# Pooled attention and rational MoE on one core: a planner with other costs and a table of due times, one-row scalars, a second home for q, 128-row last key chunk

## The chip, the cores and the metric

The kernel runs on one core of one Trainium2 chip. The metric is device time in microseconds of one execution. Engines: TensorE (PE in the profile; its weight loads are PEld), VectorE (DVE), ScalarE (ACT), GpSimd (POOL) and SyncE (SP), which here only issues DMAs.

## What is computed

```python
# q, k, v: 8 batches x 8 heads x 576 x 64, fp32
k_p = k.reshape(B, H, 72, 8, D).mean(axis=3)         # keys and values pooled by 8
v_p = v.reshape(B, H, 72, 8, D).mean(axis=3)
scores = scale * np.matmul(q, k_p.transpose(0, 1, 3, 2))
attn = np.exp(scores - np.max(scores, axis=-1, keepdims=True))
attn = attn / (np.sum(attn, axis=-1, keepdims=True) + 1e-09)
x = np.matmul(attn, v_p)                              # as 4608 tokens x 512
h = x @ w_in                                          # 512 x 2048
P = a[0] + a[1] * h + a[2] * h2 + a[3] * h3           # h2 = h*h, h3 = h2*h
Q = 1.0 + np.abs(b[0]) * np.abs(h) + np.abs(b[1]) * h2
out = (P / (Q + 1e-6)) @ w_out                        # 2048 x 512
```

## The kernel before

The 4608 tokens are 18 blocks of 256, each of two tiles of 128 tokens. The 2048 hidden columns are 8 units of 256. For a block, attention makes x in two parts (a rounded one and the remainder, since the fp32r matmul keeps fewer bits); for a block and a unit, mm1 makes h in the PSUM tile ph (24 matmuls of 128x256), rational makes gh and gl from it on ScalarE, VectorE and GpSimd, and mm2 adds them into two PSUM tiles po (12 matmuls of 128x512). Weights (win, wout) are loaded once as raw words (rwin, rwout), split into two parts on chip and kept.

In the names of the profile: st_k, st_v, and for the first two batches early, hold raw k and v; ks the pooled keys; pk (four chunks) and pl (the fifth, of 64 rows) are their transposes in PSUM, kpT the copy in SBUF. The pooled values are vm (main) and vr (the remainder of 16 rows a head), for the first two batches by matmuls with the identity, pvs and pvr. For a tile, pq is the transpose of q and qT its copy; ps the scores, mx and sm the row maximum and the sum, e the exponentials; pm and pr are transposes of e, am (hi and lo) their copies; pv the value products, x their copy. Blocks 0 to 3 transpose on TensorE; later ones on VectorE and by DMA.

The code does not issue instructions as it runs. `Plan.add` (line 125) records each with an engine, a cost in us and what it depends on. `solve` (line 166) is a list scheduler: each engine in turn takes the operation that can start first by the recorded costs and, among those within `LOOK`, the one with the least due time. Due times come from a pace of units (`due`, line 889) less a slack along the dependences. `shift` (line 158) moves the due times of some 3% of the first 1850 operations by random amounts, for each of twelve seeds. `issue` (line 252) then writes the instructions engine by engine in that order. Wherever by the plan TensorE has a gap, it fills it with matmuls of no use (line 276): into the bank idle up to a marked place, and after it, of zeros, into an open po bank. The chip keeps each engine's order and waits on semaphores, whatever the plan's times were.

Of the scalars, a and b are loaded to 128 partitions with a broadcast (line 435), and GpSimd and ScalarE make the factors abn from them (lines 437 to 440). qT has one buffer (line 634). pl is made of 64 rows (lines 511 to 514). The scores of a tile are two operations, one for each half of the heads (line 657); a tile that spans two batches (4 of the 36) has twice the matmuls, each 64 tokens wide.

## Time and profile before

| | us |
|---|---|
| median of 3 runs | 944.13 (943.72 to 944.32) |
| span of the profiled execution | 943.9 |
| TensorE busy in it | 932.3 (99%) |
| VectorE, ScalarE, GpSimd busy | 786.0, 693.7, 528.0 |

The profiled execution's own time beyond its span is not recorded; its span is 0.2 us under the median. Busy time of TensorE holds the fillers, and its matmuls are pipelined: a row's mean duration is longer than the distance of two starts.

### The profile page before, as it was taken

Reading aid. Unit: us, or ns where it says so; the run is one execution under the profiler, and the core shown is the slowest. Engines: PE = TensorE matmul, PEld = TensorE weight load, DVE = VectorE, ACT = ScalarE, POOL = GpSimd, SP = SyncE. Lnnn points to the kernel's source line nnn. Section 1 sums busy time; section 2 is a strip of 40 time slices with the busy share of each in tenths; the row PEclk is TensorE's granted clock in tenths of the full one; section 3 lists DMA queues with packets and bytes.
Section 4 is the critical chain, followed back from the end, with each engine's and each line's share of the span. In section 5 each row is a group of like instructions: output and inputs, shape, how many; then the busy total and the mean of one; then the engine's idle time right before and its main releaser. Section 6 shows DMA issues by size and latency. Waiting matters only on the chain.

```text
span 943.9 us, 17079 instructions
## 1 busy us (share of the span) xinstructions
PE 932.3 (99%) x6152; PEld 845.0 (90%) x6152; DVE 786.0 (83%) x1336; ACT 693.7 (73%) x1124; POOL 528.0 (56%) x463
## 2 busy tenths in 40 slices
PE   8899999999999999999999999999999999999998
PEld 8888998989988899998999899998999899999996
DVE  7799988788989888887887997888898987887664
ACT  4788889868675877686776777676868595868674
POOL 4776866866446544445634574447545663544443
PEclk9999999999999999999999999999999999999999
DMA  9994201254235322122603160316222421202000
GB/s 275 313 390 160 45 29 46 67 127 87 49 81 105 86 34 47 29 56 53 138 5 75 51 140 8 54 37 139 47 36 50 97 50 28 51 1 57 1 23 23
DMA packets 185365, 75.33 MB, mean 80 GB/s; under 512 B 162624, under 2 KB 162624, under 8 KB 185280
## 3 DMA queue, kind: packets, MB, share of 16 engines
q1 hardware_dynamic: 185280, 74.23, 31.2%
q8 instruction: 49, 0.80, 0.4%
q14 instruction: 36, 0.29, 0.1%
HBM read 50.60 MB, written 12.58 MB: 67 GB/s over the span
## 4 chain that ended last, share of the span: by engine, by line
PE 87%; DMA 3%; SPq 3%; DVE 3%; POOL 1%; ACT 1%; issue 1%; POOLq 0%; ACTq 0%
PE ph L284 39%; PE po L284 39%; PE pv L284 4%; PE ps L284 4%; SPq L284 3%; DMA q<-in_q_dram 1%; DMA early<-in_v_dram 1%; DVE sm L284 1%; DMA st_v<-in_v_dram 1%; DVE t L284 1%; POOL w L284 0%; PE pvs L284 0%; ACT rp L284 0%; PE pq L284 0%; DVE mx L284 0%
## 5 line engine op out<-in xcount | busy, mean ns | idle before, releaser
L284 PEld LDWEIGHTS ph<-x,win 128*128 128x128 f32 x3264 | 472.7, 188 | 55.5 <-ACT w L284 0.8
L284 PE MATMUL ph<-x,win 128*128 128x256 f32 x3264 | 495.7, 282 | 1.4 <-DVE x L284 0.5
L284 PE MATMUL po<-wout,gh 128*128 128x512 f32 x1152 | 353.1, 397 | 0.1
L284 POOL TENSOR_TENSOR w<-w,r 128x512 f32<-128x512 f32 (+1 forms) x145 | 191.1, 1318 | 230.3 <-ACT r L284 228.1
L284 POOL TENSOR_TENSOR gl<-t,gh 128x512 fp32r<-128x512 f32 (+1 forms) x145 | 193.3, 1333 | 93.1 <-ACT gh L284 91.9
L284 PEld LDWEIGHTS po<-wout,gh 128*128 128x128 f32 x1152 | 185.7, 189 | 12.5 <-POOL wout L284 0.8
L284 PE MATMUL po<-wout,gl 128*128 128x512 f32 x576 | 181.8, 396 | 0.3 <-POOL gl L284 0.3
L284 ACT ACTIVATE rp<-w,cbias 128x512 f32<-128x512 f32 (+1 forms) x145 | 99.6, 687 | 59.8 <-POOL w L284 56.6
L284 DVE SCALAR_TENSOR_TENSOR t<-t,abn,rp 128x512 f32<-128x512 f32 (+1 forms) x145 | 107.3, 740 | 38.4 <-ACT rp L284 35.3
L284 DVE TENSOR_TENSOR t<-t,ph 128x512 f32<-128x512 f32 (+1 forms) x145 | 97.8, 675 | 48.7 <-ACT t L284 46.7
L284 ACT ACTIVATE r<-w,abn 128x512 f32<-128x512 f32 (+1 forms) x145 | 117.9, 813 | 20.8 <-POOL gl L284 11.4
L284 ACT ACTIVATE t<-ph,abn 128x512 f32<-128x512 f32 (+1 forms) x145 | 111.0, 767 | 26.3 <-PE ph L284 23.0
L284 ACT ACTIVATE w<-ph 128x512 f32<-128x512 f32 (+1 forms) x145 | 85.7, 591 | 40.8 <-PE ph L284 34.4
L284 DVE SCALAR_TENSOR_TENSOR t<-t,abn,ph 128x512 f32<-128x512 f32 (+1 forms) x145 | 107.0, 738 | 5.2 <-ACT w L284 1.3
L284 ACT CAST gh<-t 128x512 fp32r<-128x512 f32 (+1 forms) x145 | 88.3, 609 | 20.5 <-DVE t L284 16.9
L284 DVE SCALAR_TENSOR_TENSOR t<-rp,t 128x512 f32<-128x512 f32 (+1 forms) x145 | 99.4, 685 | 4.1
L284 DVE SCALAR_TENSOR_TENSOR rp<-w,rp 128x512 f32<-128x512 f32 (+1 forms) x145 | 99.0, 683 | 0.2
L284 PEld LDWEIGHTS po<-wout,gl 128*128 128x128 f32 x576 | 93.0, 189 | 6.4 <-POOL gl L284 0.5
L284 ACT ACTIVATE rp<-rp 128x512 f32<-128x512 f32 (+1 forms) x145 | 84.1, 580 | 3.6 <-DVE t L284 0.5
L284 POOL TENSOR_TENSOR e<-e,sm 128x576 f32<-128x576 f32 x36 | 41.8, 1175 | 51.2 <-DVE sm L284 38.7
L284 POOL TENSOR_TENSOR st_v<-st_v 128x512 f32<-128x512 f32 (+1 forms) x36 | 36.3, 1015 | 17.4 <-DMA st_v<-in_v_dram 10.7
L284 PE MATMUL ps<-kpT,qT 128*128 128x144 f32 (+1 forms) x320 | 45.6, 292 | 0.4 <-DVE kpT L284 0.2
(101 smaller groups left out, 855.9 us busy)
## 6 DMA issues: line engine op xcount, KB each, us to landing
am<-e SPq DMA_DIRECT2D x224, 48.0 KB, 2.1
out_dram<-ob SPq DMA_DIRECT2D x17, 512.0 KB, 3.1
rwin<-in_moe_w_in_dram SPq DMA_DIRECT2D x8, 1024.0 KB, 11.1
rwout<-in_moe_w_out_dram SPq DMA_DIRECT2D x8, 1024.0 KB, 14.1
st_k<-in_k_dram SPq DMA_DIRECT2D x12, 512.0 KB, 4.8
st_v<-in_v_dram SPq DMA_DIRECT2D x12, 512.0 KB, 4.2
q<-in_q_dram SPq DMA_DIRECT2D x144, 32.0 KB, 2.0
st_v<-in_v_dram SPq DMA_DIRECT2D x48, 64.0 KB, 2.2
```

What stands on the lines that cost most here:

```text
L284: getattr(engines[op.eng], name)(*map(value, args), **{k: value(v) for k, v in kw.items()})
```

## The change

The planner's costs are set anew: a lower fixed cost for VectorE and ScalarE (0.16 and 0.17 to 0.068 and 0.06), GpSimd 0.14 and 2.15 ns an element instead of 0.45 and 1.72, TensorE's costs by the operation; a result is ready `TAIL` after its operation's end and `HOP` later on another engine; loads move at 410 instead of 390 GB/s. `shift` uses a table, `LATER`, of due times by the operation's number, and `HOLD` gives seven operations an earliest start in the plan; both replace the random seeds. The attention of blocks 1 to 3 gets a due time 8 or 10 us earlier. a and b are loaded as one row each; a matmul with a row of ones, ab, spreads them over 128 partitions. The second tile's qT of blocks 0 and 1 lies in a part of early. The lower 64 rows of the last key chunk's ks are set to zero and all 128 rows are transposed. A two-batch tile's scores are one operation.

```diff
 class Plan:
-    LAT = 0.07
-    BEGIN = {"sp": 0.8, "pe": 1.7, "pool": 1.3, "dve": 1.5, "act": 1.5}
+    TAIL = {"sp": 0.0, "pe": 0.16, "pool": 0.06, "dve": 0.09, "act": 0.1}
+    HOP = {"sp": 0.035, "pe": 0.035, "pool": 0.08, "dve": 0.035, "act": 0.035}
+    BEGIN = {"sp": 0.8, "pe": 2.1, "pool": 1.3, "dve": 1.5, "act": 1.5}
-    MOVED, SHARE, REACH = 1850, 0.03, 4.0
-    SHIFTS = (600170, 650652, 293686, 721265, 222299, 972752, 932340, 238443, 467684, 409349, 642869, 707107)
+    RATE = 410e3
+    LATER = {
+        40: -21840.4, 45: -7931.8, 50: -6005.5, 61: -3867.9, 77: -7203.6, 85: -2.3, 99: -5839.5,
...
+    HOLD = {
+        80: 10.7, 85: 12.91, 94: 18.34, 135: 28.4, 183: 31.95, 216: 29.1, 458: 52.15,
+    }
     def shift(self):
+        for n, us in self.LATER.items():
+            self.ops[n].due += us
     def solve(self):
+            op.ready = max(op.ready, self.HOLD.get(op.seq, 0.0))
...
-                op.end = bus + 2.2
+                op.done = bus + 2.2
...
+                if u.eng != op.eng:
+                    u.ready = max(u.ready, op.done + u.lead + self.HOP[u.eng])
+                elif op.eng == "pe":
+                    u.ready = max(u.ready, op.end + u.lead)
+                else:
+                    u.ready = max(u.ready, op.done + u.lead + 0.03)
...
-    dve = Engine(plan, "dve", 0.16, 1.04)
-    act = Engine(plan, "act", 0.17, 0.85)
-    gp = Engine(plan, "pool", 0.45, 1.72)
+    dve = Engine(plan, "dve", 0.068, 1.04)
+    act = Engine(plan, "act", 0.06, 0.85)
+    gp = Engine(plan, "pool", 0.14, 2.15)
...
     def scalars():
-        dma(2, ab[:, 0:4], a.partition_broadcast(P))
-        dma(1, ab[:, 4:6], b.partition_broadcast(P))
+        small("memset", line, 1.0)
         for i in range(4):
-            small("tensor_scalar", out=abn[:, i:i + 1], in0=ab[:, i:i + 1],
-                                scalar1=-WS ** -i, scalar2=None, op0=ALU.mult)
-        act(6).activation(abn[:, 4:6], ab[:, 4:6], AF.Abs)
+            small("memset", scale[:, i:i + 1], -WS ** -i)
+        dma(0.02, ab[:, 0:4], a.unsqueeze(0))
+        dma(0.02, ab[:, 4:6], b.unsqueeze(0))
+        every = bank("ab", [P, 6])
+        pe(220, [mm(every, line, ab, True, True)])
+        dve(4).tensor_tensor(out=abn[:, 0:4], in0=every[:, 0:4], in1=scale[:, 0:4], op=ALU.mult)
+        act(6).activation(abn[:, 4:6], every[:, 4:6], AF.Abs)
...
-            ks = new("work1", "ks", [P, 2, 2, D], F32, f"ks{n}_{c0}")[:np, 0:nc_]
+            every = new("work1", "ks", [P, 2, 2, D], F32, f"ks{n}_{c0}")
+            ks = every[:np, 0:nc_]
+            if np < P:
+                gp(2 * D).memset(every[np:, 0:nc_], 0.0)
...
-                ("transpose", (pk[:, (c0 + c) * P:(c0 + c + 1) * P] if c0 < 4 else pl[:, 0:np],
-                               ks[:, c].rearrange("p a d -> p (a d)"), ident[:np, :np]), {})
+                ("transpose", (pk[:, (c0 + c) * P:(c0 + c + 1) * P] if c0 < 4 else pl,
+                               every[:, c].rearrange("p a d -> p (a d)"), ident), {})
...
-        qT = new("work1", "qT", [P, NJ * P], F32, f"qT{t}").rearrange("p (j t) -> p j t", j=NJ)
+        qT = (early(t // 2, 1)[:, RW:2 * RW] if t in (1, 3) else
+              new("work1", "qT", [P, NJ * P], F32, f"qT{t}")).rearrange("p (j t) -> p j t", j=NJ)
...
+        scores = [bank(f"ps{t}_{c}", [P, 4, SP]) for c in range(2)]
+        calls = [mm(scores[c][r0:r1, 2 * jj:2 * jj + 2, :], qT[:, 2 * c + jj, r0:r1],
+                    kpT[n % 2][:, 2 * c + jj, :], True, True)
+                 for c in range(2) for jj in range(2) for r0, r1, n in sg]
+        for part in [calls] if len(sg) > 1 else [calls[:2], calls[2:]]:
+            pe(1350 if len(sg) > 1 else 244 * 2, part, claims=(e, mx, sm))
...
+            plan.now = due(at) - (0 if again else {1: 8, 2: 10, 3: 10}.get(i, 0.0))
             xs[i, again] = reload(i, kept.pop(i)) if again else attend(i)
```

TensorE in the head, before: from the last scores of tile 1 to the first value products (pvs, pvr: pooled values of the first batch; idle x22: fillers).

```order
L284 MATMUL ps_0_258<-kpT_99,qT_243 128x144 x2
L284 MATMUL pvs_263<-early_2_116,identr 128x256 x8
L284 MATMUL pvr_289<-early_1_103,fourfold 128x128 x8
L284 MATMUL pm_308<-identr,e_240 128x128 x4
L284 MATMUL pm_316<-identr,e_240 128x128 x4
L276 MATMUL idle<-identr 128x256 x2
L284 MATMUL pr_331<-identr,e_240 128x128 x2
L276 MATMUL idle<-identr 128x256 x2
L284 MATMUL pr_344<-identr,e_240 128x128 x2
L276 MATMUL idle<-identr 128x256 x22
L284 MATMUL idle<-identr 128x128
L284 MATMUL pq_390<-identr,q_256 128x128 x4
```

The same place after.

```order
L307 MATMUL ps_0_249<-kpT_99,early_1_110 128x144 x2
L307 MATMUL pvs_258<-early_2_120,identr 128x256 x8
L299 MATMUL idle<-identr 128x256 x6
L307 MATMUL pm_290<-identr,e_252 128x128 x4
L299 MATMUL idle<-identr 128x256 x13
L307 MATMUL pvr_326<-early_1_110,fourfold 128x128 x8
L307 MATMUL pm_345<-identr,e_252 128x128 x4
L307 MATMUL pr_352<-identr,e_252 128x128 x2
L307 MATMUL idle<-identr 128x128
L307 MATMUL pr_365<-identr,e_252 128x128 x2
L307 MATMUL pv_0_375<-am_0_300,vm_295 128x256
```

pvr moves behind the first pm and 13 fillers, and the value products pv come ahead of the transpose of q of the next block. In all, fillers go from 66 into idle and 10 into po to 50 into idle and none into po. After the value products the new order has one transpose of q, four ph matmuls, and then the next block's scores between ph matmuls; the old one had the scores of both tiles ahead of ph.

SP's loads in the head, before.

```order
L284 DMA early_2_116<-in_v_dram 128x4x512
L284 DMA rwin_121<-in_moe_w_in_dram 128x4x512
L284 DMA early_1_103<-in_v_dram 16x2x512 x2
L284 DMA rwin_145<-in_moe_w_in_dram 128x4x512
L284 DMA ab<-in_moe_b_dram 128x2
L284 DMA ab<-in_moe_a_dram 128x4
L284 DMA rwout_214<-in_moe_w_out_dram 128x2x1024
L284 DMA q_256<-in_q_dram 128x8x64 x2
L284 DMA rwin_286<-in_moe_w_in_dram 128x4x512
L284 DMA early_0_299<-in_k_dram 128x2x512 x2
```

The same place after (fourfold is the buffer that now holds the one row of a and b).

```order
L307 DMA early_2_120<-in_v_dram 128x4x512
L307 DMA rwin_127<-in_moe_w_in_dram 128x4x512
L307 DMA rwin_134<-in_moe_w_in_dram 128x4x512
L307 DMA early_1_110<-in_v_dram 16x2x512 x2
L307 DMA fourfold<-in_moe_a_dram 1x4
L307 DMA rwin_204<-in_moe_w_in_dram 128x4x512
L307 DMA rwout_216<-in_moe_w_out_dram 128x2x1024
L307 DMA q_254<-in_q_dram 128x8x64 x2
L307 DMA early_0_309<-in_k_dram 128x2x512
L307 DMA fourfold<-in_moe_b_dram 1x2
```

The remainder of v moves behind the second w_in, a third w_in moves ahead of q, and b goes behind the first half of the next k.

TensorE at the tile that spans batches 2 and 3, before: the second half of its scores, ps_1; the first half, ps_0, stands above it, with pl and eight po matmuls between.

```order
L284 MATMUL po_0_0_3207<-wout_2092,gl_5_3528 128x512
L284 MATMUL po_0_1_3209<-wout_2092,gl_5_3528 128x512
L284 MATMUL po_0_0_3207<-wout_2092,gh_5_3507 128x512
L284 MATMUL po_0_1_3209<-wout_2092,gh_5_3507 128x512
L284 MATMUL ps_1_3610<-kpT_99,qT_3559 64x144
L284 MATMUL ps_1_3610<-kpT_205,qT_3559 64x144
L284 MATMUL ps_1_3610<-kpT_99,qT_3559 64x144
L284 MATMUL ps_1_3610<-kpT_205,qT_3559 64x144
L284 MATMUL ph_0_3620<-x_5_3501,win_386 128x256 x8
```

The same tile after: its scores stand together.

```order
L307 MATMUL ps_0_3596<-kpT_99,qT_3564 64x144
L307 MATMUL ps_0_3596<-kpT_153,qT_3564 64x144
L307 MATMUL ps_0_3596<-kpT_99,qT_3564 64x144
L307 MATMUL ps_0_3596<-kpT_153,qT_3564 64x144
L307 MATMUL ps_1_3601<-kpT_99,qT_3564 64x144
L307 MATMUL ps_1_3601<-kpT_153,qT_3564 64x144
L307 MATMUL ps_1_3601<-kpT_99,qT_3564 64x144
L307 MATMUL ps_1_3601<-kpT_153,qT_3564 64x144
L307 MATMUL po_0_0_3221<-wout_1952,gh_5_3550 128x512
```

What moved: the second half of the scores, up to the first, at three of four such tiles (at the first one both halves already stood together).

## Rows read from the trace of the kernel before

**Rows 1.** The page's first line: span of the profiled execution.

```profile
span 943.9 us, 17079 instructions
```

**Rows 2.** Busy us by stage: PE, PEld, DVE, ACT, POOL (counts), PEclk, DMA share, GB/s.

```profile
0.00:30.30 30.30, 26.35 (x183) 24.49 (x184) 21.13 (x47) 14.71 (x29) 16.36 (x53) 1.00 0.90 278
30.30:100.00 69.70, 67.30 (x478) 60.29 (x477) 60.96 (x100) 59.24 (x98) 52.11 (x36) 1.00 0.78 265
100.00:900.00 800.00, 799.13 (x5269) 726.31 (x5269) 679.68 (x1153) 593.69 (x953) 442.57 (x360) 1.00 0.27 59
```

**Rows 3.** TensorE's groups by shape: count | busy us, mean ns | idle before.

```profile
L276 PE MATMUL idle<-identr 128*128 128x256 f32 x66 | 11.3, 323 | 0.0
...
L276 PE MATMUL po<-zero,identr 128*128 128x256 f32 x10 | 1.7, 282 | 0.0
```

**Rows 4.** TensorE's timeline, head and a wait: start us, us, instruction [idle before <-releaser].

```profile
17.29 2.05 PE L284 MATMUL pvr<-early,fourfold 32*128 32x128 f32 x16
...
25.60 0.63 PE L284 MATMUL pq<-identr,q 128*128 128x128 f32 x4 [1.49 <-DMA q<-in_q_dram]
...
27.00 1.15 PE L284 MATMUL ps<-kpT,qT 128*128 128x144 f32 x8
27.99 0.60 PE L284 MATMUL pq<-identr,q 128*128 128x128 f32 x4
...
30.31 2.38 PE L284 MATMUL ph<-x,win 128*128 128x256 f32 x18
...
41.48 0.27 PE L284 MATMUL pv<-am,vm 128*128 128x256 f32 x1
42.15 0.44 PE L284 MATMUL pk<-identr,ks 128*128 128x128 f32 x2 [0.40 <-POOL ks L284]
```

**Rows 5.** TensorE's timeline around pk, pl and the narrow scores.

```profile
61.93 1.20 PE L284 MATMUL ps<-kpT,qT 128*64 128x144 f32 x16
63.06 0.50 PE L284 MATMUL ph<-x,win 128*128 128x256 f32 x2
...
434.54 0.64 PE L284 MATMUL ph<-x,win 128*128 128x256 f32 x4
435.01 0.62 PE L284 MATMUL po<-wout,gl 128*128 128x512 f32 x2
435.48 0.38 PE L284 MATMUL pk<-identr,ks 128*128 128x128 f32 x2
435.61 0.72 PE L284 MATMUL ph<-x,win 128*128 128x256 f32 x4
...
639.85 0.63 PE L284 MATMUL ph<-x,win 128*128 128x256 f32 x4
640.42 0.27 PE L284 MATMUL pl<-identr,ks 64*128 64x64 f32 x1
640.62 0.73 PE L284 MATMUL po<-wout,gh 128*128 128x512 f32 x2
...
740.75 0.63 PE L284 MATMUL po<-wout,gh 128*128 128x512 f32 x2
741.31 0.71 PE L284 MATMUL ps<-kpT,qT 128*64 128x144 f32 x8
741.95 0.51 PE L284 MATMUL ph<-x,win 128*128 128x256 f32 x2
```

**Rows 6.** VectorE's, then ScalarE's timeline in the head.

```profile
20.12 1.22 DVE L284 SCALAR_TENSOR_TENSOR m_win<-rwin,m_win 128x1024 int32<-128x1024 int32 x1
21.25 1.28 DVE L284 TENSOR_TENSOR am<-pm,am 128x512 fp32r<-128x512 f32 x2
22.55 0.77 DVE L284 TENSOR_TENSOR am<-pr,am 64x256 fp32r<-64x256 f32 x2
...
21.91 1.21 ACT L284 ACTIVATE m_win<-rwin 128x1024 f32<-128x1024 f32 x1
...
27.20 0.59 ACT L284 CAST x<-pv 128x512 fp32r<-128x512 f32 x1 [0.25 <-PE pv L284]
```

More of the change, by code (lines that the diff above doesn't have):

```diff
@@ L97 @@
     __slots__ = ("eng", "cost", "port", "calls", "deps", "users", "bufs", "due", "wait",
-                 "ready", "seq", "bytes", "early", "slack", "start", "end", "lead")
+                 "ready", "seq", "bytes", "early", "slack", "start", "end", "done", "lead")
 class Plan:
-    LAT = 0.07
-    BEGIN = {"sp": 0.8, "pe": 1.7, "pool": 1.3, "dve": 1.5, "act": 1.5}
+    TAIL = {"sp": 0.0, "pe": 0.16, "pool": 0.06, "dve": 0.09, "act": 0.1}
+    HOP = {"sp": 0.035, "pe": 0.035, "pool": 0.08, "dve": 0.035, "act": 0.035}
+    BEGIN = {"sp": 0.8, "pe": 2.1, "pool": 1.3, "dve": 1.5, "act": 1.5}
     WARM = 8.6
     LOOK = 0.02
-    MOVED, SHARE, REACH = 1850, 0.03, 4.0
-    SHIFTS = (600170, 650652, 293686, 721265, 222299, 972752, 932340, 238443, 467684, 409349, 642869, 707107)
+    RATE = 410e3
+    LATER = {
[12 rows of a table added]
+    }
+    HOLD = {
+        80: 10.7, 85: 12.91, 94: 18.34, 135: 28.4, 183: 31.95, 216: 29.1, 458: 52.15,
+    }
     def __init__(self, nc):
@@ L230, in solve @@
                 op.end = t + 2 * op.cost
+            op.done = op.end + self.TAIL[op.eng]
             at[op.eng] = op.end
@@ L234, in solve @@
             if op.bytes:
-                bus = max(bus, op.end) + op.bytes / 390e3
-                op.end = bus + 2.2
-                flights = sorted(flights[1:] + [op.end])
+                bus = max(bus, op.end) + op.bytes / self.RATE
+                op.done = bus + 2.2
+                flights = sorted(flights[1:] + [op.done])
             for b in op.bufs:
                 b.left -= 1
-                b.it = max(b.it or 0.0, op.end)
+                b.it = max(b.it or 0.0, op.done)
                 if not b.left:
@@ L244, in solve @@
                 u.wait -= 1
-                u.ready = max(u.ready, op.end + u.lead + (self.LAT if u.eng != op.eng else 0.0))
+                if u.eng != op.eng:
[4 more added lines that the diff above has]
+                    u.ready = max(u.ready, op.done + u.lead + 0.03)
                 if not u.wait:
@@ L395, in small @@
     def small(name, *args, **kw):
-        plan.add("pool", 0.2, [(name, args, kw)])
+        plan.add("pool", 0.13, [(name, args, kw)])
     def make_masks():
@@ L427, in tile_pooled_attention_then_rational_moe @@
     CW = 2 * DM
-    ab = new("cpool", "ab", [P, 6], F32, "ab")
+    scale = new("cpool", "ab", [P, 6], F32, "ab")
     abn = new("cpool", "abn", [P, 8], F32, "abn")
@@ L659, in attention @@
             js = slice(2 * c, 2 * c + 2)
-            ps = bank(f"ps{t}_{c}", [P, 4, SP])
-            pe(245 * 2 * len(sg), [
-                mm(ps[r0:r1, 2 * jj:2 * jj + 2, :], qT[:, 2 * c + jj, r0:r1],
-                   kpT[n % 2][:, 2 * c + jj, :], True, True)
-                for jj in range(2) for r0, r1, n in sg], claims=(e, mx, sm))
+            ps = scores[c]
             dve(4 * SP).tensor_reduce(out=mx[:, hs], in_=ps, op=ALU.max, axis=AX.X)
@@ L908, in tile_pooled_attention_then_rational_moe @@
             plan.slack = 1.4
+            plan.now = due(at) - (0 if again else {1: 8, 2: 10, 3: 10}.get(i, 0.0))
             xs[i, again] = reload(i, kept.pop(i)) if again else attend(i)
+            plan.now = due(at)
             plan.slack = 1.4
```

29 lines of the change are left out of this document (12 added, 17 removed), and 11 rows, old and new, of the table LATER.

## The prediction

> **What bounds the kernel now.** I read the span first [rows 1], then the busy time by stage [rows 2], then TensorE's groups by shape [rows 3], then its timeline around the waits [rows 4, 5] and last the engines that feed it in the first 30 us [rows 6]. From 100 to 900 us TensorE is busy 799.13 of 800 us at a granted clock of 1.00, the 2.4 GHz level [rows 2]: two po matmuls take 0.47 us and four ph matmuls 0.47 us [rows 5], and nothing but fewer or cheaper matmuls shortens that stage. Before 30.3 us it is idle for 3.95 us and from 30.3 to 100 for 2.4 us [rows 2], and part of what counts as busy is filler: 66 matmuls into the idle bank and 10 into po, all before 100 us [rows 3]. So three things can move the end: what TensorE pays for odd shapes, how soon the first ph starts, and what it loses between then and 100 us. The rest of the run only passes this on.
>
> **Odd shapes.** The pl transpose of 64 rows: the ph matmuls before it hold it off 0.57 us where four take 0.47, so it enters 0.10 late; it lasts 0.20 to the next start; and the po pair behind it shows 0.73 us against 0.62, another 0.10 [rows 5]. Together 0.40 us. Two pk transposes of 128 rows start 0.13 us apart from what follows, whose row is 0.08 longer: 0.21 for two, 0.11 for one [rows 5]. The change makes pl one of 128 rows, 0.29 us less each. Eight are run, one of them in the head, where fillers stood on both sides: 7 x 0.29 = 2.0 us. The cost is a memset of the lower half of ks on GpSimd for each, which shares its buffer's release with the adds before it; the new wait is TensorE's on that memset, with all ph and po behind it. GpSimd is idle nearly half the time, and I price it at 0, at most 0.1 us each (0.8).
>
> The scores of a tile that spans two batches: a half of eight narrow matmuls enters 0.10 us late (po pair at 740.75, next start 741.31), lasts 0.64 and leaves 0.10 later: 0.84 us, twice 1.68. The one tile where both halves already stood together took 1.13 + 0.20 = 1.33 us [rows 5]. In the old order three of four such tiles are split, in the new one none: 3 x 0.35 = 1.05 us.
>
> Here the Trainium skill has a rule (TensorEngine Tiling (Array Packing), Key Properties): a change of tiling mode drains the engine. The 0.10 us on either side of pl and of the narrow scores agree with it, but the value products do not: vr's matmuls use 64 columns between vm's of 128, and the row at 41.48 follows one without a gap [rows 4]. By the rule the ab matmul, of one row, pays both drains, 0.3 us in all; by the pv rows 0.1, and the sum would be 0.2 less.
>
> **The scalars.** Two broadcast loads become two one-row loads, a matmul ab and two copies out of its bank. Four small GpSimd steps go; they end long before the first ph needs them. The ab matmul stands between ph matmuls. No row has one of one row; the nearest are pl at 0.40 and a pk at 0.11. I take 0.3. Behind it stand the rest of ph for the first two units and the next scores. What it may wait for is b, now queued on SP behind the first half of the second batch's k; by my chain below ab is reached some 5 us after the first ph, so I price the wait at 0 and let it reach 2 us.
>
> **The head.** The first ph stood at 30.31 us, but by then TensorE had also done the scores of tiles 2 and 3, two groups of 0.99 [rows 4] and two transposes of q, four times 0.11 each by the price of pk, 2.9 us. Without them it would have stood at 27.4. The new order starts ph after one such transpose (0.44), so it must start before 27.9 to be earlier. I follow the new order with the old durations. The scores of tiles 0 and 1 now stand together, so the softmax is ready somewhat sooner, but pvr, which ran at 17.29 in the softmax's shadow [rows 4], now comes after the first pm and 13 fillers, because the remainder of v is queued behind a second w_in. One such load is 1.05 MB, at 278 GB/s [rows 2] 3.8 us at most, since other loads share that rate. I take pvr at 19.1 (bounds 17.3 and 21.1), and with 2.0 us its end is 21.1. Then VectorE has, before the third pv matmul can go, the weight step of 1.22, two steps of pr at 0.39, two of vr that I price alike, and am of tile 1 at 0.64 [rows 6]: 3.4 us, to 24.5. Sixteen pv matmuls at 0.118 end at 26.4; ScalarE's last cast for x takes 0.59 [rows 6], and the weight step that stands ahead of the first cast holds it up by some 0.4: 27.4. The transpose of q also comes before ph; its load moves behind one more w_in but ahead of no broadcasts. Before, TensorE waited 1.49 us for it at 25.60 [rows 4]; I let it land between 25.5 and 29.3 and take it as not later than 27. So ph at 27.8 with its transpose, as late as before for the same work: I take 0, bounds -2 and +2.
>
> **From the first ph to 100 us.** The idle time is 2.4 us [rows 2], but a shown wait understates the loss: at 42.15 the row shows 0.40 us idle, while the starts lie 0.67 apart where 0.12 is the pace [rows 4], 0.55 lost. By that ratio, 1.4, 2.4 us of idle time cost 3.4. The ten po fillers add 10 x 0.12 = 1.2 us, and the order after has none of them; nothing else comes in their places but ph, since three w_in are loaded ahead of the second batch's k and a third unit's ph is there to fill. The waits are on e, ks and am. The planner's new costs fit the rows better: a VectorE step of 512 elements lasts 0.64 us [rows 6], the old costs hold the engine 0.69 for it, the new ones 0.60 with the result 0.09 later. So the order should ask for results when they exist; but it was planned with loads at 410 GB/s, and the stretches here move 265 to 278 [rows 2]. I let a third of the waits stay, 3.4 x 2 / 3 + 1.2 = 3.5 us gained, bounds 0 (each wait replaced by another) and 4.6.
>
> **After 100 us.** Idle time is 0.87 us from 100 to 900 [rows 2]; the order there is new everywhere and the last 40 TensorE rows are the same. I take 0, bounds -2 and +1.
>
> **Sum.** 943.9 - 2.0 - 1.05 + 0.3 - 0 - 3.5 = 937.65. The runs' median is 944.13, 0.2 above the profiled span, so 937.9 in the runs' measure.
>
> **Rivals.**
> 1. Only the shapes are gained: loads move between, the waits of the ramp return under other names and the fillers turn into idle time. For it speaks that SP's loads are the same megabytes in another order and that one transpose of q and pvr now wait for later places; against it that the third w_in is ahead, so ph work is there. 944.1 - 3.05 + 0.3 = 941.4, with a head 1 us later 942.4.
> 2. The ramp runs nearly without waits: both upper bounds, 2 us in the head and 4.6 behind it: 944.1 - 2.75 - 6.6 = 934.75; with the idle time after 100 us also gone 933.9. For it speaks that three units' ph are there to fill with; against it that every load is still the same size.
> 3. Slower: the value products come too early in every block. TensorE runs in order, so a pv matmul that waits for am on VectorE holds ph and po behind it; the row at 42.15 shows what 0.40 us of such a wait costs, 0.55. If the tighter plan does this in each of the 18 blocks, it costs 9.9 us, and 937.9 + 9.9 = 947.8. It decides from 6.2 / 18 = 0.34 us lost in each block on. Against it: between 100 and 900 us, 14 blocks, only 0.87 us of idle time stands.
> 4. The clock: without the fillers TensorE stands idle in the head and falls to the lower of its two levels. At 25.60 it had waited 1.49 us and the stretch up to 30.3 kept 1.00 [rows 2, 4], so a gap of that size does not do it. If it fell to 1.2 GHz, each us of work then done takes two; for 2 to 4 us of work the price is 2 to 4 us: 940 to 942.
> [...] No row of the kernel before shows such a fall.
>
> **Numbers.** Forecast 937.9: chance 0.60, its own range 935.5 to 940.5. Rival 1: 0.17, rival 2: 0.13, rival 3: 0.06, rival 4: 0.04. The range of 8 in 10 takes the forecast and most of rivals 1 and 2: 933.8 to 942.3. About 0.2%, 1.9 us, is what a measurement can tell from no change: same is 942.2 to 946.0. Faster gets 0.60 + 0.13 + 0.13 of rival 1 + 0.04 = 0.90, same 0.05 (the rest of rival 1 and the small end of 3), slower 0.05.
>
> **What would show it.** Eight pl rows of 128x128 with about 0.11 us between their start and the next. Narrow scores in four runs of sixteen at about 1.13 us. Sixty fillers or fewer and none into po. The first ph between 26 and 29.5 us, with one transpose of q just ahead of it, and its wait, if any, on DMA q. Idle time from there to 100 us of about 0.8 us; 2.4 or more says rival 1, none says rival 2. The 100 to 900 stretch busy for 799 us. Wrong would be: a wait on ab's load, a granted clock under 1.00 past the first 6 us, or pv rows that wait for am in block after block.

## The result and the profile after

The changed kernel takes 947.96 us (median of 6 runs, 945.93 to 949.46) against 943.98 (6 runs, 943.28 to 944.32): a ratio of 1.0040, interval 1.0028 to 1.0051. It is slower, where 937.9 was forecast. Three of its six runs had a mean granted clock of 1.0 and took 945.93, 946.32 and 947.48; three had 0.998 or 0.999 and took 948.44 to 949.46. Even the three at 1.0 lie above all six runs of the kernel before. The profiled run is one of the latter three, the slowest; its span stands against 943.9 [rows 1]. In the executions of the kernel before that were timed beside the experiments, the time is 1.7 to 1.8 us beyond the span, and the median span is 942.2 to 942.7: the execution of [rows 1] was longer than most, by some 1.5 us, and a difference of two profiles is that uncertain.

```profile
span 946.8 us, 17070 instructions
```

Busy us by stage, columns as in [rows 2]:

```profile
0.00:20.00 20.00, 17.43 (x104) 16.24 (x105) 13.07 (x34) 7.68 (x14) 9.88 (x53) 1.00 0.97 302
20.00:30.30 10.30, 8.56 (x55) 7.80 (x55) 7.24 (x11) 7.89 (x16) 6.53 (x3) 0.83 1.10 340
30.30:100.00 69.70, 67.88 (x486) 61.25 (x485) 64.54 (x111) 58.85 (x103) 49.82 (x36) 1.00 0.73 241
100.00:900.00 800.00, 797.28 (x5248) 720.77 (x5247) 662.63 (x1144) 587.36 (x948) 438.81 (x365) 1.00 0.26 60
```

Two things differ from before. The clock column has 0.83 between 20 and 30.3 us, where it was 1.00, and from 100 to 900 us TensorE is idle for 2.72 us, where it was 0.87 [rows 2]. Its waits of 0.6 us and more, summed by what they wait for (us in total, times, longest; left out is the first filler's wait for identr, 2.2, before 2.1):

```profile
PE ps L307 <- DVE qT L307: 1.5, 2, 1.3
PE pv L307 <- DVE am L307: 1.3, 1, 1.3
PE pm L307 <- DVE t L307: 0.7, 1, 0.7
PE ph L307 <- DVE x L307: 0.7, 1, 0.7
PE ph L307 <- DVE t L307: 0.6, 1, 0.6
PE ps L307 <- ACT qT L307: 0.6, 1, 0.6
```

All but one of these lines name VectorE; am and x are known from before, qT, t ahead of pm and t ahead of ph are new or larger. TensorE's timeline in the head, where [rows 4] showed the kernel before:

```profile
23.22 0.33 PE L307 MATMUL pr<-identr,e 128*128 128x128 f32 x1 [0.35 <-ACT e L307]
23.30 0.48 PE L307 MATMUL pv<-am,vm 128*128 128x256 f32 x2
25.05 0.33 PE L307 MATMUL pv<-am,vr 128*64 128x256 f32 x1 [1.27 <-DVE am L307]
25.21 0.62 PE L307 MATMUL pv<-am,vm 128*128 128x256 f32 x3
...
27.76 1.06 PE L307 MATMUL pq<-identr,q 128*128 128x128 f32 x4
28.47 0.91 PE L307 MATMUL ph<-x,win 128*128 128x256 f32 x4
...
34.41 0.38 PE L307 MATMUL ab<-fourfold 1*128 1x6 f32 x2
34.72 3.97 PE L307 MATMUL ph<-x,win 128*128 128x256 f32 x32
```

The first ph stands at 28.47, behind one transpose of q. The clock right after the wait for am is the lower level, 1.2 GHz:

```profile
25.50:28.80 3.30, 3.30 (x17) 3.30 (x17) 0.87 (x2) 1.83 (x3) 1.87 (x1) 0.50 1.06 341
```

The shapes came as forecast. In TensorE's groups, columns as in [rows 3], no filler goes into po and 50 of this shape (66 before) go into idle, and the pl rows are eight of 128x128. In its timeline behind them pl lasts 0.02 to the next start, and the narrow scores are sixteen in a row, 1.13 us between starts (543.86 to 544.99), where [rows 5] had 0.84 for each half:

```profile
L299 PE MATMUL idle<-identr 128*128 128x256 f32 x50 | 9.7, 360 | 0.0
L307 PE MATMUL pl<-identr,ks 128*128 128x128 f32 x8 | 2.3, 282 | 0.3 <-DVE ks L307 0.2
```

```profile
446.00 0.27 PE L307 MATMUL pl<-identr,ks 128*128 128x128 f32 x1
446.02 0.71 PE L307 MATMUL ph<-x,win 128*128 128x256 f32 x4
...
543.86 1.20 PE L307 MATMUL ps<-kpT,qT 128*64 128x144 f32 x16
544.99 0.75 PE L307 MATMUL ph<-x,win 128*128 128x256 f32 x4
```

The largest new wait is at 693. TensorE's rows come first, then VectorE's, then ScalarE's; the last two rows are the same scores and their qT in the kernel before, without a wait:

```profile
691.34 0.63 PE L307 MATMUL po<-wout,gh 128*128 128x512 f32 x2
693.25 0.64 PE L307 MATMUL ps<-kpT,qT 128*128 128x144 f32 x3 [1.28 <-DVE qT L307]
...
690.74 0.69 DVE L307 TENSOR_TENSOR t<-t,ph 128x512 f32<-128x512 f32 x1 [1.21 <-ACT t L307]
691.46 0.75 DVE L307 SCALAR_TENSOR_TENSOR t<-t,abn,ph 128x512 f32<-128x512 f32 x1
...
692.49 0.70 DVE L307 STREAM_TRANSPOSE qT<-q 128x512 f32<-128x512 f32 x1
...
688.92 0.62 ACT L307 CAST gh<-t 128x512 fp32r<-128x512 f32 x1 [2.22 <-DVE t L307]
689.45 0.59 ACT L307 ACTIVATE w<-ph 128x512 f32<-128x512 f32 x1
689.94 0.77 ACT L307 ACTIVATE t<-ph,abn 128x512 f32<-128x512 f32 x1
...
689.30 0.76 PE L284 MATMUL ps<-kpT,qT 128*128 128x144 f32 x4
688.54 0.71 DVE L284 STREAM_TRANSPOSE qT<-q 128x512 f32<-128x512 f32 x1
```

Read the changed kernel's rows from below: ScalarE's cast gh waits 2.22 us with the next unit's w and t queued behind it, VectorE's steps of t wait for that t, qT is queued behind them, and TensorE waits for qT. In the plan qT was done 0.17 us before TensorE wanted it.

**A mark in the run.** Both kernels run the same 5184 long products (3456 ph, 1728 po), and at the start of the 400th (before: 118.49 us, after: 117.94) they have nearly the same other work left. I split every profile there; the whole head lies ahead of it, and in these two kernels all fillers do. Up to there the change gained 0.55 us; behind it the kernel before needs 825.4 us and the changed one 828.9. So the loss is behind the mark, where I had forecast a gain by the shapes. Single profiles scatter: three kernels with the changed kernel's order there, but for one cast, took 828.9, 829.8 and 829.0. Counted from start to start behind the mark, against 118 and 231.5 ns for a long product, the difference lies at:

```
scores (matmuls and waits for them)   27.8 -> 30.2    +2.4, though their shapes gave back 0.7
ph behind a po (waits)                 0.5 ->  2.2    +1.7
ph behind a ph (waits, exits of scores) 2.1 -> 3.8    +1.7
po behind a ph                         1.1 ->  0.0    -1.1
pl                                     1.6 ->  0.4    -1.2
pk, po behind po, pv                  39.2 -> 39.5    +0.3
```

The sum is 3.8 for 3.4, since the changed kernel has three po more done at the mark and three ph less, which leaves it 0.34 us less of long products behind it.

### The profile page after: what moved, and what is told of

It is laid out like the page before. It is cut to its first block, busy times and chain, and to the rows that moved or that the text cites. A ratio compares the mean times of both kernels' runs of the same rounds, so it can differ in the third digit from the quotient of the medians.

```text
span 946.8 us, 17070 instructions
## 1 busy us (share of the span) xinstructions
PE 933.3 (99%) x6128; PEld 842.0 (89%) x6128; DVE 772.5 (82%) x1337; ACT 688.6 (73%) x1124; POOL 524.1 (55%) x472
## 4 chain that ended last, share of the span: by engine, by line
PE 80%; DVE 8%; ACT 4%; POOL 3%; issue 2%; DMA 2%; SPq 1%; DVEq 0%; ACTq 0%; POOLq 0%
PE ph L307 36%; PE po L307 36%; PE pv L307 4%; PE ps L307 3%; DVE t L307 3%; POOL gl L307 1%; DVE sm L307 1%; DVE rp L307 1%; DVE e L307 1%; POOL w L307 1%; ACT rp L307 1%; SPq L307 1%; DVE mx L307 1%; DMA early<-in_k_dram 1%; POOL st_v L307 1%
## 5 line engine op out<-in xcount | busy, mean ns | idle before, releaser
L307 PEld LDWEIGHTS ph<-x,win 128*128 128x128 f32 x3264 | 479.4, 189 | 62.2 <-DVE x L307 1.1
L307 PE MATMUL ph<-x,win 128*128 128x256 f32 x3264 | 503.2, 282 | 1.5 <-DVE x L307 0.7
L307 POOL TENSOR_TENSOR gl<-t,gh 128x512 fp32r<-128x512 f32 (+1 forms) x145 | 190.6, 1314 | 54.7 <-ACT gh L307 49.6
L307 PEld LDWEIGHTS po<-wout,gh 128*128 128x128 f32 x1152 | 183.2, 188 | 10.2 <-ACT gh L307 0.6
L307 PE MATMUL pv<-am,vm 128*128 128x256 f32 (+3 forms) x288 | 46.6, 282 | 0.0
L307 PEld LDWEIGHTS ps<-kpT,qT 128*128 128x128 f32 (+1 forms) x304 | 36.1, 178 | 9.7 <-DVE qT L307 4.1
```

The lines of the kernel that those rows point to most:

```text
L307: getattr(engines[op.eng], name)(*map(value, args), **{k: value(v) for k, v in kw.items()})
```

## The experiments

All of them in one table; the short diffs and what follows come below. "Ratio" is against runs of the kernel before on the same chip (medians 943.9 to 944.4). The last two columns come from the profiled run: us up to the 400th long product, and from there to the end.

| kernel | us (runs) | ratio (95%) | to 400th | from 400th |
|---|---|---|---|---|
| before | 943.98 (6) | 1 | 118.5 | 825.4 |
| after | 947.96 (6) | 1.0040 (1.0028 to 1.0051) | 117.9 | 828.9 |
| fill_pv | 947.43 (5) | 1.0036 (1.0023 to 1.0050) | 115.9 | 829.8 |
| old_order_pl128 | 945.15 (11) | 1.0007 (0.9998 to 1.0016) | 117.6 | 826.3 |
| dve_moved | 947.15 (11) | 1.0027 (1.0017 to 1.0037) | 116.0 | 827.4 |
| pe_slow | 956.90 (4) | 1.0123 (1.0107 to 1.0140) | 118.1 | 836.3 |
| old_order_ks | 943.06 (11) | 0.9988 (0.9979 to 0.9996) | 116.2 | 824.5 |
| before_no_table | 947.73 (3) | 1.0040 (1.0024 to 1.0055) | 122.0 | 824.0 |
| after_no_table | 952.38 (4) | 1.0086 (1.0072 to 1.0100) | 123.6 | 827.5 |
| pe_slow_no_table | 958.69 (3) | 1.0144 (1.0128 to 1.0159) | 129.0 | 828.0 |
| after_old_costs | 948.76 (3) | 1.0058 (1.0043 to 1.0073) | 122.9 | 824.2 |
| after_old_engines | 959.76 (3) | 1.0162 (1.0146 to 1.0178) | 124.3 | 833.8 |
| before_new_costs | 949.92 (3) | 1.0068 (1.0053 to 1.0084) | 120.7 | 826.9 |
| refit_old_costs | 946.82 (5) | 1.0035 (1.0023 to 1.0048) | 121.4 | 824.0 |
| after_new_rules | 955.06 (3) | 1.0115 (1.0099 to 1.0130) | 123.5 | 829.9 |
| after_old_rules | 972.76 (3) | 1.0301 (1.0285 to 1.0317) | 123.5 | 847.5 |
| after_old_dve | 953.37 (2) | 1.0096 (1.0077 to 1.0114) | 121.0 | 829.7 |
| old_order_moved | 943.32 (11) | 0.9991 (0.9982 to 1.0000) | 117.3 | 824.0 |
| act_moved | 947.80 (5) | 1.0035 (1.0022 to 1.0049) | 116.8 | 829.0 |

**fill_pv: the clock.** Twelve fillers ahead of the first two pv matmuls, behind which TensorE waited for am; nothing else moved.

```diff
+ for _ in range(12): nc.tensor.matmul(<bank of pv0_0>, lhsT=filler, rhs=one, start=True, stop=True)
  <first pv step of the first tile>
```

> The changed kernel with twelve fillers more, written into the bank of the first value products ahead of them, where TensorE waited 1.43 us (starts at 23.5 us of the changed kernel's profile); nothing else moves. Theory (clock): the gaps of the head let the granted clock fall to 1.2 GHz for 3.4 us in some executions, and that costs some 2 us there. With the fillers no execution shows the fall: clock 1.00 in all, times near the lower runs of the changed kernel, 945.9 to 946.5. Rival 1 (the fall has another cause, or its time is given back): times stay at 946 to 949.5, median about 948. Rival 2 (fillers end late and push the value products): clock 1.00 and about 947.5.

In TensorE's timeline the gap is filled, and in the row of the stretch (columns as in [rows 2]) the clock stays at 1.00:

```profile
22.93 1.67 PE L306 MATMUL pv<-identr 128*128 128x256 f32 x12
24.43 0.40 PE L313 MATMUL pv<-am,vm 128*128 128x256 f32 x2
...
26.72 0.98 PE L313 MATMUL ph<-x,win 128*128 128x256 f32 x4
```

```profile
20.00:30.00 10.00, 9.65 (x77) 8.84 (x76) 7.98 (x13) 8.28 (x15) 6.56 (x3) 1.00 1.10 338
```

The first ph comes 1.75 us sooner and the mark 2.1 us sooner, but the time is 947.43, inside the range of the changed kernel. The five runs took 946.65 to 950.2, four of them with a mean clock of 1.00 and the slowest with 0.999, so the theory's 945.9 to 946.5 was missed. Rival 2's number came, but not by its mechanism: the first two pv come later (24.43 for 23.30), yet the first ph comes sooner, so nothing is pushed on. So the fall of the clock is real, and without it and the gap the mark comes some 2 us sooner, but it does not explain why the kernel is slower where it does not happen.

**old_order_pl128, old_order_ks: the transpose alone.** The kernel before, its order kept. First with the lower half of ks set to zero in the same step on the same engine:

```diff
+    ([("memset", (every[np:, 0:nc_], 0.0), {})] if np < P else []) +
     [("tensor_tensor", (), dict(out=ks, ...
-    pl[:, 0:np], ks[:, c], ident[:np, :np]
+    pl, every[:, c], ident
```

> The kernel before with its own order of instructions, and pl transposed with 128 rows: the lower half of ks is set to zero in the step that writes the upper half, on the same engine. Theory (the price of the shape is right and is not given back): 7 x 0.29 = 2.0 us less than the kernel before, 942.0. Rival (other engines set the pace of TensorE, so time saved in one place is waited for in the next): less than 0.7 us off, 943.3 to 944.

The gain is missing: 945.15, longer than either theory or rival had it. The memset stands ahead of ks on VectorE, and TensorE now waits for what comes behind it (for kpT 0.9 us on VectorE, where it was 0.2), at 538.47 for ks itself:

```profile
537.66 0.63 PE L284 MATMUL po<-wout,gh 128*128 128x512 f32 x2
538.47 0.33 PE L284 MATMUL pl<-identr,ks 128*128 128x128 f32 x1 [0.19 <-DVE ks L284]
```

Then without any memset: one fixed home for ks, whose lower rows hold finite sums of the chunk ahead; their columns of pl nobody reads.

```diff
+    ks = real([P, 2, 2, D], F32, tag="ks", name="ks")
-    ks = new("work1", "ks", [P, 2, 2, D], F32, f"ks{n}_{c0}")[:np, 0:nc_]
-    pl[:, 0:np], ks[:, c], ident[:np, :np]
+    pl, ks[:, c], ident
```

> The kernel before, instruction for instruction in its old order on every engine; the sums of each key chunk lie in one fixed home, so that the last chunk's transpose is of 128 rows (rows 64 to 127 hold finite sums of the chunk ahead, whose columns nobody reads) and no memset is needed. Theory A (the shape gain is real and reaches the end where nothing else is added; in the run with the repeated memset the two late waits for ks on VectorE ate it): 944.0 - 2.0 = 942.0, at most 942.8, ratio 0.997 to 0.999. Rival B (a shorter step ahead of a wait only makes the wait longer, whatever the shape): 943.5 to 944.5, ratio 0.9995 to 1.0005, with the time back in scores that wait for kpT.

943.06 against 944.3: ratio 0.9988, so 0.4 to 2.0 us faster. Where [rows 5] had 0.40 us for pl, the rows now hold 0.03 from pl's start to the next, and 0.08 in the row behind:

```profile
637.51 0.28 PE L284 MATMUL pl<-identr,ks 128*128 128x128 f32 x1
637.54 0.71 PE L284 MATMUL po<-wout,gh 128*128 128x512 f32 x2
```

The shape gain was right, and it reaches the end when nothing is added ahead of ks. Of the 2.0 us forecast the median shows 1.2; of the 2.3 us by which its profile is sooner at the mark, the one pl that lies there can explain only 0.3.

**pe_slow and the tables.** The changed kernel with TensorE's two long products planned 1% slow, as before:

```diff
-  last = pe(118.1 * n, [
+  last = pe(119.5 * n, [
-  return pe(231.6 * len(ms), [
+  return pe(233 * len(ms), [
```

> The changed kernel with the planner's costs for mm1 and mm2 as they were before, 119.5 and 233 ns a matmul instead of 118.1 and 231.6; the whole order is planned anew. Theory (slack): a plan in which TensorE is 1% slower than the chip has every other engine's results ready early, so small delays are taken up; TensorE's idle time from 100 us to the end falls from 5.4 us (rows of the changed kernel, by stage) to under 3.5, and the time to 943 to 945.5. Rival 1 (the waits come from collisions and loads that no pace of TensorE covers): idle time stays at 4.5 to 6.5 and the time at 946 to 948.5. Rival 2 (an order is one draw out of many and the table was chosen for the other paces): longer than the changed kernel, 949 or more.

956.9, in rival 2's range: my theory that the plan only lacked slack on TensorE is wrong as tried. Next, each kernel with its table empty (`SHIFTS = ()`, or `LATER, HOLD = {}, {}`), and pe_slow too.

> The kernel before with its random shifts of due times empty. The planner's own end rises from 946.6 to 950.6 us. Theory A (the planner's gain carries to the chip): 944.0 + 3.9 = 947.9, 946.5 to 949.5. Rival B (it exists in the planner alone): 943 to 945. If A holds here and not for the changed kernel, the old costs foretell the chip's order better than the new ones.

> The changed kernel with both tables of due times and holds empty; all other parts of the change stand, and everything is planned anew. The planner's own end rises from 927.3 to 930.1 us. Theory A (what the planner's order gains in its own arithmetic carries to the chip): 947.96 + 2.8 = 950.8, 949 to 952.5. Rival B (an order planned to the true paces leaves VectorE's transposes late whatever the table says, and the table's gain of 2.8 us exists in the planner alone): 946 to 949, no different from the changed kernel. Rival C (the table itself does the harm, it packs the order without slack): 942 to 945.

> The changed kernel with TensorE's two long products at the old costs (119.5 and 233 ns) and with the tables empty. The planner's own end is 940.3 us (934.6 with the tables, which came to 956.9 on the chip). Theory A (planner's gain carries): 956.9 + 5.7 = 962.6. Rival B (the tables were fitted to the other costs and did the harm of that run; without them a plan with 1% of slack on TensorE does as the kernel before): 943 to 947. Rival C (the order is a draw, no cost or table foretells it within 5 us): anything from 945 to 960.

Both tables help on the chip: 3.7 us of planned 3.9 for before, 4.4 of 2.8 for after, 1.8 of 5.7 for pe_slow. Nearly all of it lies ahead of the mark (122.0 to 118.5, 123.6 to 117.9); behind it before and after lose 1.4 each, and pe_slow 8.3 (828.0 to 836.3): most of what made it slow there goes with the tables, which were chosen for the other costs. So the table is not what makes the change slow; without tables it is 4.7 us slower than before as well. And the planner's own end ranks orders only under one set of paces: 946.6 came to 944.0, 927.3 to 948.0.

**Paces or the other parts.** Without tables: the kernel before with the new paces, the change with the old ones, and the change with only VectorE's, ScalarE's and GpSimd's costs old.

```diff
-    dve = Engine(plan, "dve", 0.068, 1.04)
-    act = Engine(plan, "act", 0.06, 0.85)
-    gp = Engine(plan, "pool", 0.14, 2.15)
+    dve = Engine(plan, "dve", 0.16, 1.04)
+    act = Engine(plan, "act", 0.17, 0.85)
+    gp = Engine(plan, "pool", 0.45, 1.72)
```

> The kernel before, no shifts, planned with the change's paces on all engines and no other part of the change. The planner's own end falls from 950.6 to 929.7 us. Theory A (the new paces lose the time): 947.7 + 4.7 (952.4 against 947.7) + 1.2 (64-row transposes) = 953.6, 951 to 956. Rival B (other parts): 946.5 to 949, as without the new paces. Rival D (the chip follows the planner's own end): 927 to 935.

> The changed kernel with all its parts but the planner's paces: costs, ends and hops of all engines as in the kernel before, no table. The planner's own end is 948.9 us. Theory A (the new paces lose the time): the old paces foretold the chip 2.6 and 2.8 us too long, with and without shifts (946.6 and 944.0, 950.6 and 947.7), and the 128-row transpose gave 1.2 beyond the plan, so 948.9 - 2.7 - 1.2 = 945.0, 943.5 to 946.5. Rival B (the other parts lose it: the row of a and b, q's other home, both halves of the scores in one step, first tiles due sooner): 951 to 953, as the changed kernel without tables (952.4).

> The changed kernel without its tables, with only the costs of VectorE, ScalarE and GpSimd as in the kernel before (0.16, 0.17 and 0.45 us for each instruction, for 0.068, 0.06 and 0.14); TensorE's paces, the hops and the ends of steps stay as in the change. The planner's own end rises from 930.1 to 950.5 us by these alone. Theory A' (it is the overhead of these three engines' instructions, whose slack the changed plan lost): 950.5 - 2.7 - 1.2 = 946.6, 944.5 to 948.5. Rival A'' (it is TensorE's true pace or the hops): 951 to 953.

In whole times the new paces cost 2.2 us on the old parts (947.7 to 949.9) and 3.6 on the new (948.8 to 952.4); by the ratios 0.28% each, 2.6 us. Both expectations of 945 and 953.6 were missed, and both times lie between the theory's range and the rival's. The column behind the mark tells more: with the old paces 824.0 and 824.2 whatever the parts are, with the new 826.9 and 827.5. (That the new parts' shapes, forecast at 2.75 us there, show in neither pair is not explained; in after_old_costs 13 fillers behind the mark take 1.5 of it.) The rest of the whole times is the head (120.7 to 123.6), where every order without a table differs and the clock falls in three of these four profiles. The mixed set, old costs on three engines and new ones on TensorE, is worse than either (833.8) and outside both expectations. But there the planner saw gaps and put 71 fillers behind the mark, 8.0 us from start to start; if nothing had waited in their place, the stretch would have taken 825.7.

**refit_old_costs.** The change's parts with the old paces and eight random seeds of shifts, chosen for the planner's end.

```diff
+    SHIFTS = (158176, 48845, 669949, 122783, 983005, 19613, 111263, 918963)
```

> The changed kernel's parts (row of a and b, 128-row transposes, q's other home, scores in one step, first tiles sooner) with the old paces on all engines, and eight random shifts of due times chosen for the planner's own end, which is 944.1 us (946.6 for the kernel before). Theory A (under one set of paces what the planner gains carries, 3.9 planned and 3.7 measured for the kernel before): 944.1 - 2.7 - 1.2 = 940.2, 938.8 to 942, ratio 0.994 to 0.998. Rival C (any order is a draw): 943 to 950.

946.82: missed. Behind the mark it has the good 824.0, but its head took 121.4, at a granted clock of 0.95 from 15 to 50 us. That what the planner gains carries to the chip held for one table and not for this one.

**Which of the paces.** Costs and rules (when a result counts as there) crossed, and VectorE's cost alone:

```diff
-    TAIL = {"sp": 0.0, "pe": 0.16, "pool": 0.06, "dve": 0.09, "act": 0.1}
-    HOP = {"sp": 0.035, "pe": 0.035, "pool": 0.08, "dve": 0.035, "act": 0.035}
+    TAIL = dict.fromkeys(("sp", "pe", "pool", "dve", "act"), 0.0)
+    HOP = dict.fromkeys(TAIL, 0.07)
```

> The changed kernel without tables; costs of all engines as in the kernel before, TensorE's too; only the rules for when a step's result counts as there (its end plus 0.06 to 0.16 us, hops of 0.035 or 0.08, 0.03 within an engine) are the change's. Planner's own end 958.0 us. Read from the 400th of the long products to the end of the profile, which took 824.0 to 825.4 us in every run with the old paces whatever else was changed, and 826.9 to 829.8 with the new. Theory E (the engines' costs alone make the later stretch long): 824 to 825.5 here. Theory R (the rules make it): 826.9 to 830. The whole time: 948 to 950 by E, 951 to 955 by R.

> The mirror of the last: the changed kernel without tables with the old rules (0.07 us between engines, nothing else) and the new costs of all engines. Planner's own end 930.0 us. From the 400th long product to the end: theory E 826.9 to 830, theory R 824 to 825.5. The whole time: 951 to 954 by E, 947 to 950 by R.

> The changed kernel without tables, with VectorE's cost alone as before (0.16 us an instruction for 0.068), all else new. Planner's own end 934.3 us. Theory V (what runs late in the later stretch is VectorE's transposes of q and its steps for TensorE, so its cost alone mends it): 824 to 826 from the 400th long product on, 949 to 950.5 whole. Rival (a plan with one engine slower than its neighbours is worse than either pure set, as the two mixed ones were, 833.8 and 836.3): 828 to 836 for that stretch, 953 to 960 whole.

(The expectation says that all runs with the old paces took 824.0 to 825.4 behind the mark; old_order_pl128, with its memset, had 826.3.) Behind the mark: old costs and old rules 824.2, old costs and new rules 829.9, new costs and old rules 847.5, both new 827.5. These numbers do not settle it as they stand, for in after_new_rules 43 fillers lie behind the mark, 5.2 us from start to start, 13 of them here:

```profile
171.18 1.62 PE L283 MATMUL po<-zero,identr 128*128 128x256 f32 x13
```

For at least 3.3 us of this, by the trace, what the next matmul waits for was already there. Without them the stretch would take between 824.7, if nothing else waited, and 829.9; no run shows it. Theory R is out, since the old rules with the new costs came to 847.5 and not to 824 to 825.5. Theory E missed there too (826.9 to 830), but its other half, 824 to 825.5 with the old costs, may hold but for the fillers. My reading, which no run tests by itself, is that the two belong together: the old fixed cost of 0.16 us held the delay that the new rules add on their own, so old costs with new rules count it twice, and the planner fills gaps that the chip need not have; new costs with old rules count it nowhere. That set, after_old_rules, is by far the worst: the row below is its longest wait, and VectorE's qT there stands behind a sum that waits for a load. In this profile the clock also falls to 0.50 three times behind the mark, for 13.7 us, in which TensorE is busy some 12.4; an estimate from that is 6 us of the 23 over 824.2.

```profile
709.09 0.63 PE L291 MATMUL po<-wout,gh 128*128 128x512 f32 x2
714.00 0.85 PE L291 MATMUL ps<-kpT,qT 128*128 128x144 f32 x2 [4.29 <-DVE qT L291]
...
712.23 0.73 DVE L291 TENSOR_TENSOR st_k<-st_k 64x256 f32<-64x256 f32 x2 [1.21 <-DMA st_k<-in_k_dram]
...
713.25 0.69 DVE L291 STREAM_TRANSPOSE qT<-q 128x512 f32<-128x512 f32 x1
```

after_old_dve has no filler behind the mark and took 829.7 there, 953.37 in all: in the rival's ranges, so VectorE's cost alone does not mend it.

**Single waits taken away.** In the changed kernel, three instructions of VectorE that TensorE waits for, moved ahead of others:

```diff
+        self.sooner("qT29", 3)
+        self.sooner("qT19", 1)
+        self.sooner("x1_3", 2)
```

> The changed kernel with three of VectorE's steps moved ahead of one to three steps of the rational chain: the transposes qT of tiles 29 and 19 and x's second half of block 3, for which TensorE waited 1.44, 0.42 and 0.85 us. Theory (each of these waits is a local fault of the order, and the run only passes it on): the three waits are gone and the run is 2.0 to 2.7 us shorter than the changed kernel, some 945.5 at the median. Rival (VectorE and ScalarE are the pace there, and the steps that now come later are waited for): under 0.8 us off, 947.2 to 948.

The three waits go or shrink, and the stretch behind the mark falls from 828.9 and 829.8 to 827.4 in the profiled run; in the median the whole falls by 0.8, to 947.15, where the theory had 945.5 and the rival 947.2 to 948. The profiled run is the fastest of the eleven, and the intervals of the two kernels overlap, so no gain is shown. qT is now done by 688.84, but the second half of these scores waits for a step of t that was put behind it:

```profile
688.90 0.76 PE L324 MATMUL ps<-kpT,qT 128*128 128x144 f32 x4
690.35 0.73 PE L324 MATMUL ps<-kpT,qT 128*128 128x144 f32 x4 [0.69 <-DVE t L324]
```

Then the same place by ScalarE's order instead:

```diff
  <ScalarE, near 689 us>
-  CAST gh
   ACTIVATE w<-ph
   ACTIVATE t<-ph,abn
+  CAST gh
```

> The changed kernel, its tables too, with one instruction of ScalarE moved: near 689 us its cast gh stands two places later, behind w and t of the next unit. In the changed kernel the cast waits 2.22 us for VectorE's t there, w and t behind it come late, so VectorE's steps t come late, and qT, queued behind them, after TensorE asks for it (1.28 us idle at 693.25). Theory Q (a step that waits at the head of an in-order queue hands its delay to the next engines): the wait for qT there falls from 1.44 us lost to under 0.4, the rest stays; from the 400th long product on 827.4 to 828.7 (828.9 and 829.8 in the two runs with this order), whole 945.5 to 947.5. Rival S (qT is late because VectorE's sum of st_k beside GpSimd took 1.49 us at 680.57, or of itself): the wait stays over 1 us.

```profile
691.40 0.63 PE L330 MATMUL po<-wout,gh 128*128 128x512 f32 x2
692.29 0.88 PE L330 MATMUL ps<-kpT,qT 128*128 128x144 f32 x5 [0.26 <-DVE qT L330]
...
687.41 0.80 ACT L330 ACTIVATE t<-ph,abn 128x512 f32<-128x512 f32 x1
689.26 0.62 ACT L330 CAST gh<-t 128x512 fp32r<-128x512 f32 x1 [1.06 <-DVE t L330]
```

The wait shrinks from 1.28 us to 0.26 (1.44 to 0.42 lost), 0.02 over what I had set as the bound: ScalarE's order handed most of it on. Rival S is out: the sum of st_k still takes 1.47 us, at 680.93. The whole does not gain: 829.0 behind the mark and 947.8, both over the expectation. In this profile a new wait of 1.34 stands at 537.83, told in the last section. Last, two such moves in the kernel before with old_order_ks:

```diff
+        self.sooner("x1_0", 1)
+        self.sooner("am1_5", 1)
```

> The kernel before in its old order with the 128-row transposes and the fixed home of the key sums (943.06, its best version so far), and two instructions of VectorE one place sooner: the add for x that TensorE waited 0.58 us for at 30.6, ahead of a sum of e; the add for am that it waited 0.96 us for at 279.7, ahead of a step of t. If a wait that goes is kept to the end: 943.06 - 0.5 - 0.7 = 941.9 (941 to 942.6), ratio 0.996 to 0.999. If the moved work only comes back as waits of the steps that it passes: 943.0.

Both waits are gone from the profile (the first returns as a longer wait for e, 0.85 us ahead of 34.34), and the stretch behind the mark has the least time of all, 823.99, but the median is 943.32, no better than 943.06. So old_order_ks is the version that beats both kernels, by about 0.1%, and a wait taken away by hand added nothing to it that can be measured.

## Why the prediction was wrong

**Right.** The shapes: pl at 0.11 us and the narrow scores at 1.13, as worked out. They gained 1.2 us of pl behind the mark, and 1.2 (0.4 to 2.0) alone on the old order. No filler in po. The first ph within 26 to 29.5, behind one transpose. No wait on the load of b. One small miss: the ab matmuls are two and cost 0.50 us (0.31 from the first one's start to the next ph, 0.10 more on either side) where I took 0.3.

**The step that failed: "After 100 us ... I take 0, bounds -2 and +1."** With the shapes that lie there, 2.75 us were to be gained behind 100 us; behind the mark 3.4 were lost (4.4 in fill_pv). I noted that the order there was new everywhere and priced it by the old order's 0.87 us of idle time, as if little waiting were a property of the stage. It was a property of the old order. With the old paces six kernels, of four separate plans, took 823.99 to 825.4 there (826.3 with the memset of old_order_pl128); with the whole of the new, six, of three plans, took 826.9 to 829.8. My sentence that the new costs fit the rows better is true of the rows, but it does not follow that the order is better: the planner's end fell to 927.3, the chip came 20.7 us later than that, where it had come 2.6 us sooner than the old plan.

**The ramp, -3.5, with the head at 0.** Up to the mark, with 0.3 for pl and +0.3 for ab, 3.5 us were forecast; 0.55 came in the profiled run, 1.7 to 2.6 in act_moved, dve_moved and fill_pv, whose clock stayed up. The waits did return under other names (am 1.27, t 0.7, qT 0.6), which was rival 1's mechanism. The idle times that I priced were also read from an execution some 1.5 us longer than most of its kind.

**Rival 4, the clock, was dismissed by a wrong argument.** From 1.49 us of waiting without a fall [rows 2, 4] I concluded that a gap of that size does not do it. With gaps that cost 0.57 and 1.43 us from start to start it fell to 0.50 in the changed kernel's profile, and with 0.58 and 1.42 in act_moved's it did not. The runs at full clock (945.9 to 947.5) and below (948.4 to 949.5) differ by some 2.4 us in the mean, in act_moved by 1.0. The row from 25.5 to 28.8 has TensorE busy for all of 3.30 us at 0.50, which is an estimate of 1.65 us lost, half of that. So the price forecast, 2 to 4 us, was about right or somewhat high, and rival 4 happened beside the main loss. The Trainium skill (TensorE: Matmul & The Clock Gate, What's actually happening) has the fall after an idle stretch. In the changed kernel's profile it comes behind idle time, but with work between the waits, and the profiles do not show what decides between two runs of like gaps.

**Rival 3 had the right sign and nearly the right time, 947.8, by another mechanism.** It asked for one wait for am in every block. That the number came near is luck. The measured loss is a handful of waits of 0.2 to 1.5 us on qT, x, t and gl. Which steps of the new order bring each of them is shown for one only, the cast gh at 689.

**Open.** That the new paces bring the loss is shown by exchanging them in both directions, without tables. Why the pair of new costs and new rules is 3 us worse behind the mark than the old pair is not settled. The rules alone are ruled out; the costs alone are not, since the crossed runs hold fillers and falls of the clock.

## What to carry to other kernels

A list scheduler's costs are one set: change fixed costs and latency rules together, and measure the order that results, for a model that fits single instructions better can order them worse. Before two plans are compared, count what the planner itself has put in: here fillers made up to 8 us of a stretch. A plan's own end ranks tables under one set of costs and says little across two. When a change replans a stage that hardly waits, price the new order's waits there by the spread of orders, not by the waits of the old one.

## What the runs showed of the hardware

The new wait in act_moved comes from a step of VectorE with two inputs in SBUF beside a step of GpSimd. Up to 688 us every engine has the same order in act_moved and in the changed kernel, so the moved cast does not bring this wait; the two runs differ in time alone. The same two instructions in both kernels, act_moved first, then the changed kernel:

```profile
536.38 1.39 DVE L330 TENSOR_TENSOR ks<-st_k 128x256 f32<-128x256 f32 x1
...
536.22 1.27 POOL L330 TENSOR_TENSOR w<-w,r 128x512 f32<-128x512 f32 x1 [3.03 <-ACT r L330]
...
537.83 0.44 PE L330 MATMUL pk<-identr,ks 128*128 128x128 f32 x2 [1.34 <-DVE ks L330]
```

```profile
537.28 0.42 DVE L307 TENSOR_TENSOR ks<-st_k 128x256 f32<-128x256 f32 x1
...
537.27 1.57 POOL L307 TENSOR_TENSOR w<-w,r 128x512 f32<-128x512 f32 x1 [3.17 <-ACT r L307]
```

Where GpSimd's w had started 0.16 us sooner, ks took 1.39 us and TensorE waited; where the two started within 0.01 us, ks took 0.42 and w 1.57 instead of 1.27. The Trainium skill (SBUF — State Buffer, Who interferes with whom) says that such a pair contends and that the order of issue decides who waits. The first pair agrees; in the second the starts lie too close to tell which was issued first. So here a shift of 0.15 us between two runs of one order decided over 0.97 us on VectorE.

Sums of st_k or ks over 1 us number 2 in the kernel before, 5 in the changed one and 16 in after_old_rules. Each of the 5 starts while a step of GpSimd runs and ends 0.28 us after it (0.55 for the one of 512 elements). They go with the costs: the nine profiles with the old costs of VectorE, ScalarE and GpSimd have 2 or 3 each, the ten others 4 to 16. That TensorE's loss behind the mark comes from these sums is not shown.
